# Attention's value product: high and low halves in one stationary block, one accumulator for a pair of heads

## The chip, the core and the metric

One core of a Trainium2 chip runs the whole program. Its engines are TensorE (matrix products; PE in the rows, and PEld for the loads of its stationary operand), VectorE (DVE), ScalarE (ACT), GpSimd (POOL) and SyncE (SP, which issues DMAs here). They run side by side and wait for each other through semaphores. Matmul results land in PSUM, a memory of eight banks of 2 KB in each of 128 partitions. The metric is device time of one execution in microseconds; shorter is better.

## The reference

Attention with a sigmoid in place of the softmax, its output laid out by token, then a mixture of experts with one expert per token, then a two-layer network:

```
scores = q @ k.T / sqrt(64) - log(448)        # 4 batches x 12 heads, 448 tokens, head size 64
attn   = 1 / (1 + exp(-scores))
x      = (attn @ v), heads side by side       # 1792 x 768
e(t)   = argmax over 8 of normalised x @ normalised expert_emb / tau
x      = gate * (relu(x @ w1[e]) @ w2[e])     # 1024 hidden
h      = x @ w_in                             # 2048 hidden
out    = (h - tanh(h)) @ w_out
```

All is float32. To keep its precision, the kernel splits a float32 operand into a rounded high part and the low rest ("h" and "l" in the names), and multiplies high x high, high x low and low x high, each as one fast matmul.

## The kernel before

The program has three stages: attention, experts, last network. The change is in attention, and in one step where the first expert group is prepared.

Two heads make a pair; there are 24 pairs (4 batches x 6). Keys lie on partitions with head 0 in rows 0 to 63 and head 1 in rows 64 to 127. The 448 keys of a head are three chunks of 128 and a rest of 64. The work is cut into 84 "slots" of 2 x 448 columns: slots of one pair hold chunk c of both heads; a joint slot, one to two pairs, holds the rests of both heads for both pairs. Seven slots make two pairs: three, the joint one, three.

For a slot `scores` (line 248) runs three products for each half (high x high, low x high, high x low; line 257) into a PSUM tile of two banks ("pq", three buffers, which the tiles of `rows` and of the routing share). In an ordinary slot the two heads' matmuls use 64 rows each and lie in different halves of the array. Then ScalarE takes the sigmoid twice: rounded to "ah" (line 264) and in full into pq (line 265). VectorE subtracts them to "al" (line 266), which frees pq.

`av` (line 268) multiplies values with attention. Its stationary block is 128 columns for two heads, of which a head's unit fills its own half, with zeros in the other (`vpads`, line 168, sets them). Three matmuls a unit (high values x ah, low values x ah, high values x al; line 280), seven units a pair, all into one bank "pav"; there are two such buffers. After the seventh the pair is copied out to "xT", on ScalarE for odd pairs (line 293) and on VectorE for even ones (line 295).

`rows` (line 297) turns xT so that tokens are on partitions, with four fp32 matmuls against an identity that has the normalised expert embedding beside it (`ien`, line 118), so that the routing logits come out in the same product (136 columns). VectorE adds the logits and copies the tokens (lines 313 to 316).

For each pair `prep` (line 204) lets VectorE round keys and queries in one instruction (line 217) and GpSimd subtract the low part; `prep_v` (line 222) lets GpSimd do the same for values in four.

TensorE's order is that of the program in this stage (`manual_schedule`): two slots of scores, then the value units of the two slots that lie four back, then what a table of slot numbers (`plan`, line 374) has due: `rows`, loads, preparation, routing. The other engines' orders are set by a scheduler with its own priorities; every engine runs its queue in order.

`columns` (line 779) prepares a group of 256 tokens for the experts: 12 transposes in three buffers, each copied out by ScalarE and subtracted by VectorE ("xl", line 795), then two transposes of the token numbers (line 800), for the first group into the free half of the last of these buffers.

## Time and profile before

| | |
|---|---|
| median of 3 runs | 1028.97 us (1028.47 to 1029.16) |
| profiled execution, its own time | 1029.54 us |
| span of its trace | 1027.8 us |
| TensorE busy | 1000.6 us, 97% |
| VectorE, ScalarE, GpSimd busy | 790.8, 555.8, 206.8 us |
| first and last sigmoid of the attention stage | 7.5 and 213.2 us |

How to read it: a row of the trace's order of time has the start, the duration, the engine, the line, the operation, output<-inputs, the shape of the stationary operand (rows*columns), the shape of what moves, and in brackets how long the engine had been idle and what ended that. "x2" at the end merges neighbours of one kind. A matmul's duration holds its way through the array; the next one starts before it ends, so the distance of two starts is what one costs.

### The profile page before, as it was taken

The numbers are of one execution on the slowest core, as the hardware profiler recorded it, in microseconds if no ns is written. First come the engines' busy times: TensorE is split into PE (matmuls) and PEld (weight loads), VectorE is DVE, ScalarE is ACT, GpSimd is POOL, SyncE is SP. The second block draws the span as 40 slices with busy tenths as digits, with TensorE's granted clock in tenths as the row PEclk, the third lists the DMA queues.
The fourth block names the chain that finished last, engine by engine and source line by source line (L and its number), as shares of the span: only waits on it lengthen the run. The fifth ranks groups of instructions, "written<-read, shape, count | busy, mean of one in ns | idle before, by whom it ended". The sixth has DMA issues, their size and how long they took to land.

```text
span 1027.8 us, 16784 instructions
## 1 busy us (share of the span) xinstructions
PE 1000.6 (97%) x6437; PEld 934.4 (91%) x6437; DVE 790.8 (77%) x1029; ACT 555.8 (54%) x692; POOL 206.8 (20%) x310
## 2 busy tenths in 40 slices
PE   7999999989999999999999999999999999999997
PEld 5777878779999999999999899999999999999997
DVE  7787677758859788889974888998897667766774
ACT  6788897866667666676653434344343332333230
POOL 7657677646301011100000000000001200000002
PEclk9999999999999999999999999999999999999999
DMA  6433434359658965965944555445534521233212
GB/s 173 131 89 114 128 85 123 103 196 354 239 184 301 334 228 213 305 222 184 309 152 151 195 170 180 146 179 184 192 116 154 200 107 66 104 123 117 99 62 107
DMA packets 83524, 175.26 MB, mean 171 GB/s; under 512 B 7639, under 2 KB 62958, under 8 KB 83438
## 3 DMA queue, kind: packets, MB, share of 16 engines
q1 hardware_dynamic: 79438, 155.56, 44.7%
q0 software_dynamic: 3840, 18.35, 5.0%
q8 instruction: 52, 0.85, 0.3%
q14 instruction: 34, 0.28, 0.1%
q10 hardware_dynamic: 160, 0.21, 0.1%
HBM read 156.68 MB, written 36.30 MB: 188 GB/s over the span
## 4 chain that ended last, share of the span: by engine, by line
issue 55%; PE 15%; POOL 2%; DMA 1%; DVE 1%; POOLq 0%; ACT 0%; DVEq 0%
PE pth L855 7%; PE pty L855 7%; POOL out_dram L529 2%; DMA xg<-x_tok,gidx 1%; PE xt L790 1%; DVE wl L846 0%; DVE ca L974 0%; DVE ca L972 0%; POOLq L1256 0%; DVE ca L968 0%; PE xt L800 0%; DVE hl L873 0%; ACT wi L794 0%; DVE ca L970 0%; POOLq L529 0%
## 5 line engine op out<-in xcount | busy, mean ns | idle before, releaser
L1125 PE MATMUL o<-wo,gh 128*128 128x384 f32 x896 | 240.3, 335 | 0.9 <-DVE acc L1138 0.7
L1074 PE MATMUL z<-yh,wi 128*128 128x512 f32 (+1 forms) x768 | 220.0, 365 | 0.4 <-PEq L941 0.4
L1125 PEld LDWEIGHTS o<-wo,gh 128*128 128x128 f32 x896 | 162.9, 188 | 2.5 <-DVE acc L1138 1.0
L1074 PEld LDWEIGHTS z<-yh,wi 128*128 128x128 f32 x768 | 141.6, 188 | 15.7 <-ACT yh L1049 0.6
L1125 PE MATMUL o<-wo,gl 128*128 128x384 f32 x448 | 150.0, 335 | 0.5 <-DVE gl L1099 0.5
L1074 PE MATMUL z<-yl,wi 128*128 128x384 f32 (+1 forms) x384 | 138.3, 364 | 0.0
L529 POOL DMA_INDIRECT out_dram<-acc,toki x14 | 16.7, 1193 | 572.0 <-DVE acc L1138 570.8
L266 DVE TENSOR_TENSOR al<-pq,ah 128x896 fp32r<-128x896 f32 x84 | 91.4, 1088 | 41.2 <-ACT pq L265 38.3
L855 PE MATMUL pth<-wi,wh 128*128 128x256 f32 x432 | 121.4, 282 | 0.9 <-DVE hl L873 0.9
L855 PE MATMUL pth<-wi,wl 128*128 128x256 f32 x432 | 121.1, 281 | 0.6 <-DVE wl L846 0.6
L855 PE MATMUL pth<-xl,wh 128*128 128x256 f32 x432 | 120.8, 280 | 0.0
L855 PE MATMUL pty<-hh,wl 128*128 128x256 f32 x416 | 117.1, 283 | 0.3 <-DVE wl L846 0.3
L855 PE MATMUL pty<-hl,wh 128*128 128x256 f32 x416 | 117.3, 284 | 0.0
L855 PE MATMUL pty<-hh,wh 128*128 128x256 f32 x416 | 116.9, 285 | 0.0
L1138 DVE TENSOR_TENSOR acc<-o,acc 128x768 f32<-128x768 f32 x97 | 92.4, 952 | 31.8 <-PE o L1125 31.6
L1098 ACT CAST gh<-r 128x896 fp32r<-128x896 f32 x32 | 30.1, 942 | 140.8 <-DVE r L1096 79.3
L264 ACT ACTIVATE ah<-pq,bias_s 128x896 fp32r<-128x896 f32 x84 | 85.5, 1018 | 35.9 <-PE pq L257 34.1
L846 DVE TENSOR_TENSOR wl<-w1raw,wh 128x768 fp32r<-128x768 f32 x72 | 68.5, 955 | 27.8 <-ACT wh L845 27.2
L1082 ACT ACTIVATE t<-z 128x896 f32<-128x896 f32 x32 | 29.4, 920 | 107.5 <-PE z L1074 66.2
L1125 PEld LDWEIGHTS o<-wo,gl 128*128 128x128 f32 x448 | 84.1, 188 | 2.2 <-DVE gl L1099 0.8
L845 ACT CAST wh<-w1raw 128x768 fp32r<-128x768 f32 x72 | 59.5, 834 | 44.1 <-PE pty L855 21.4
L265 ACT ACTIVATE pq<-pq,bias_s 128x896 f32<-128x896 f32 x84 | 83.0, 988 | 0.0
(269 smaller groups left out, 2221.2 us busy)
## 6 DMA issues: line engine op xcount, KB each, us to landing
w1raw<-in_moe_w_dram SPq DMA_DIRECT2D x36, 768.0 KB
w2raw<-in_moe_w_dram SPq DMA_DIRECT2D x27, 1024.0 KB
wi<-dwi SPq DMA_DIRECT2D x32, 768.0 KB
wo<-dwo SPq DMA_DIRECT2D x32, 768.0 KB
cr<-in_moe_w_in_dram SPq DMA_DIRECT2D x16, 768.0 KB
dwi<-cr SPq DMA_DIRECT2D x16, 768.0 KB
cr<-in_moe_w_out_dram SPq DMA_DIRECT2D x16, 768.0 KB
dwo<-cr SPq DMA_DIRECT2D x16, 768.0 KB
```

Of the source, the lines that this page charges most:

```text
L264: nc.scalar.activation(hi, pv, AF.Sigmoid, **sc)
L265: self.last_sig = nc.scalar.activation(pv, pv, AF.Sigmoid, **sc)
L266: nc.vector.tensor_tensor(lo, pv, f32(hi), ALU.subtract)
L529: i = self.nc.gpsimd.indirect_dma_start(**kw)
L845: nc.scalar.copy(wh, cols)
L846: self.last_split = nc.vector.tensor_tensor(wl, cols, f32(wh), ALU.subtract)
L855: self.last_mm = nc.tensor.matmul(pt[:, u], a[:, kk], b[:, kk], start=(n == 0), stop=(n == 3 * K - 1))
L1074: nc.tensor.matmul(z[:, G0[g] : G0[g] + GS[g]], wi[:, a, j * P : (j + 1) * P], yhl[half][g][b][:, j], start=(left[g] == 3 * NJ), stop=(lef ...
L1082: nc.scalar.activation(t, zv, AF.Square)
L1098: nc.scalar.copy(gv, r)
L1125: nc.tensor.matmul(o[:, w, :NW], a[:, u, i * P : (i + 1) * P], wo[:, b, w * NW : (w + 1) * NW], start=(n == 0), stop=(n == 3 * CH - 1),)
L1138: nc.vector.tensor_tensor(acc[i], ov, acc[i], ALU.add)
```

## The change

Values are kept as one tile of seven blocks of 2 x 64 columns: a block holds the high and the low part of one head's chunk side by side. A unit is now two matmuls (block x ah, block x al); the sum of high and low comes out in `rows`, whose identity is two stacked 64-wide ones. As the two heads' results would fall on the same partitions, the accumulator has two banks, one per head, and there is one buffer of it. The rests of a pair (block 6: head 0 in rows 0 to 63, head 1 in rows 64 to 127) are four matmuls of 64 rows. xT is copied by VectorE for every pair. `rows` has two 72-column matmuls for each of four chunks (one per head, overlapping in the 8 logit columns, where the second adds). The slots are taken in groups of 2, 2, 2 and 1, so that a block of value units belongs to one pair only. GpSimd prepares the values in five instructions. Three value buffers are kept for two, five plus two buffers of attention for six. The embedding is loaded in four DMAs, and its step comes two slots earlier. In `columns` the number transposes of the first group go before the last buffer is copied out.

```diff
-        pav2 = self.pool("aps3", 2, cx, space=PSUM)
+        pav2 = self.pool("aps3", 1, cx, space=PSUM)
-        NV, NW, NK = 2, 3, 3
+        NV, NW, NK = 3, 3, 3
...
+        self.et = et = cp.tile([P, 2, self.NJ, self.E], F32, name="emb_t")
+        for a in range(2):
+            for p in range(2):
+                nc.sync.dma_start(et[p * D : (p + 1) * D, a], self.emb[a * D : (a + 1) * D])
...
+        self.ien = ep.tile([P, NJ, 2, D + E], F32, name="ien")
+        eye = lambda k: self.ident[:, k * D : (k + 1) * D].unsqueeze(1).to_broadcast([P, NJ, D])
+        for a, (o, u) in enumerate(((0, D), (E, 0))):
+            nc.vector.tensor_tensor(self.ien[:, :, a, o : o + D], eye(0), eye(1), ALU.add)
+            nc.vector.tensor_tensor(
+                self.ien[:, :, a, u : u + E], et[:, a], sc[:, 0].unsqueeze(1).to_broadcast([P, NJ, E]), ALU.mult
+            )
...
+            g.tensor_copy(v[:, :6, 0], vr[:, 1:7])
+            g.tensor_tensor(v[:, :6, 1], vr[:, 1:7], f32(v[:, :6, 0]), ALU.subtract)
+            g.tensor_tensor(v[:, 6, 0], vr[:, 0], vr[:, 7], ALU.add)
+            g.tensor_tensor(vr[:, 0], vr[:, 0], f32(v[:, 6, 0]), ALU.subtract)
+            g.tensor_tensor(v[:, 6, 1], vr[:, 0], vr[:, 7], ALU.add)
...
+            groups += [(u, u + 1), (u + 2, u + 3), (u + 4, u + 5), (u + 6,)]
+            two = (0, 1)
+            blocks += [
+                [(u, two), (u + 1, two)], [(u + 2, two), (u + 3, (0,))],
+                [(u + 4, two), (u + 5, two)], [(u + 6, two), (u + 3, (1,))],
             ]
...
-            hi = sp.tile([P, 2, S], F32R, tag="ah", name="ah", bufs=LAG + 2)
+            t, nb = ("j", 2) if slots[u][0][1] == 2 else ("a", 5)
+            hi = sp.tile([P, 2, S], F32R, tag=t + "h", name="ah", bufs=nb)
...
-                for m, (vv, aa) in enumerate(((vh, hi), (vl, hi), (vh, lo))):
-                    nc.tensor.matmul(
-                        pav[:, :S], vo(vv), aa[:, x], start=(b0 and m == 0), stop=(e and m == 2)
-                    )
+                for m, t in enumerate(tiles[u]):
+                    if a < 2:
+                        nc.tensor.matmul(
+                            pav[:, a, :S], vo(slice(0, P), 3 * a + c // P), t[:, x], start=(c == 0 and m == 0), stop=False
+                        )
+                    else:
+                        for h in range(2):
+                            p = slice(h * D, (h + 1) * D)
+                            nc.tensor.matmul(pav[:, h, :S], vo(p, 6), t[p, x], start=False, stop=(m == 1))
...
-                    s["xT"] = xp.tile([P, S], F32, tag="xT", name="xT")
-                    if i % 2:
-                        nc.scalar.copy(s["xT"], pav[:, :S])
-                    else:
-                        nc.vector.tensor_copy(s["xT"], pav[:, :S])
+                    s["xT"] = xp.tile([P, 2, S], F32, tag="xT", name="xT")
+                    nc.vector.tensor_copy(s["xT"], pav[:, :, :S])
...
             for c in range(NCH):
-                o = (c % 2) * W
-                nc.tensor.matmul(
-                    pr[:CP, c // 2, o : o + W], xT[:, c * CP : (c + 1) * CP], self.ien[:, j], start=True, stop=True
-                )
+                for a in range(2):
+                    nc.tensor.matmul(
+                        pr[:, c, a * D : a * D + D + E], xT[:, a, c * CP : (c + 1) * CP], self.ien[:, j, a],
+                        start=(a == 0), stop=(a == 1), skip_group_check=True,
+                    )
...
-            plan(5, self.embedding)
+            plan(3, self.embedding, lambda: pav2.tile([P, 2, 512], F32, tag="av", name="emb_ss"))
...
+            for g, us in enumerate(groups):
+                for now[0] in us:
                     if now[0] < ns:
                         scores(now[0])
+                if g >= 2:
+                    for t in blocks[g - 2]:
+                        av(*t)
...
+            if jj == NJ // 2 - 1 and full.shape[2] >= 2 * GR:
+                pr = numbers(full[:1, 0, GR : 2 * GR])
             nc.scalar.copy(xh[:, js], pt)
```

TensorE's order around the end of a pair, before: the last value units ("vh", "vl" are the high and low values), rows, and the next slots' scores ("w" are keys and queries).

```order
L280 MATMUL pav<-al,vh_197 128x448
L280 MATMUL pav<-ah,vh_197 128x448
L280 MATMUL pav<-ah,vl_198 128x448
L280 MATMUL pav<-al,vh_197 128x448
L305 MATMUL pr<-ien,xT 112x136 x4
L257 MATMUL pq<-w0h 128x448 x2
L257 MATMUL pq<-w0l,w0h 128x448 x2
L257 MATMUL pq<-w0h,w0l 128x448 x2
```

The same place in the changed program ("v" is the tile with both parts; L283 are the half-height matmuls of the rests).

```order
L277 MATMUL pav<-ah,v_191 128x448
L277 MATMUL pav<-al,v_191 128x448
L283 MATMUL pav<-ah,v_191 128x448 x2
L283 MATMUL pav<-al,v_191 128x448 x2
L303 MATMUL pr<-ien,xT 112x72 x8
L258 MATMUL pq<-w2h 128x448 x2
L258 MATMUL pq<-w2l,w2h 128x448 x2
L258 MATMUL pq<-w2h,w2l 128x448 x2
```

Two matmuls a unit stand where three stood, the pair now ends with two couples of half height, and rows has eight matmuls of 72 columns for four of 136.

VectorE's order over some slots before, with one of its copies of xT:

```order
L266 TENSOR_TENSOR al<-pq,ah 128x896 x2
L315 TENSOR_TENSOR u<-pr,u 112x32
L316 COPY yT_last<-pr 112x4x128
L449 TENSOR_REDUCE mx<-lg 112x4
L217 TENSOR_REDUCE w1h<-kq_186 128x960
L456 TENSOR_REDUCE cm<-cand 112x4
L266 TENSOR_TENSOR al<-pq,ah 128x896
L295 COPY xT<-pav 128x448
L266 TENSOR_TENSOR al<-pq,ah 128x896 x2
```

And in the changed program (L214 is the rounding of keys and queries, L265 the subtraction of a slot):

```order
L265 TENSOR_TENSOR al<-pq,ah 128x896
L293 COPY xT<-pav 128x896
L265 TENSOR_TENSOR al<-pq,ah 128x896
L313 TENSOR_TENSOR u<-pr,u 112x32
L315 COPY yT_last<-pr 112x4x128
L265 TENSOR_TENSOR al<-pq,ah 128x896 x2
L313 TENSOR_TENSOR u<-pr,u 112x32
L315 COPY yT_last<-pr 112x4x128
L447 TENSOR_REDUCE mx<-lg 112x4
L214 TENSOR_REDUCE w1h<-kq_186 128x960
L293 COPY xT<-pav 128x896
L265 TENSOR_TENSOR al<-pq,ah 128x896
```

Every pair has its copy of xT here now, twice as wide; it stands ahead of the subtraction of the slot scored last, once of two times with the rounding right in front.

## Rows read from the trace of the kernel before

**Rows 1.** The page, busy time of an engine: us, share of the span, instructions.

```profile
PE 1000.6 (97%) x6437; PEld 934.4 (91%) x6437; DVE 790.8 (77%) x1029; ACT 555.8 (54%) x692; POOL 206.8 (20%) x310
```

**Rows 2.** Instructions of line 264: ns min/median/max, first and last start.

```profile
L264 ACT ACTIVATE ah<-pq,bias_s x84: 991/1011/1115, 7.5 to 213.2; 128x896 fp32r<-128x896 f32 x84
```

**Rows 3.** Waits from 20 to 180 us: total us, times, longest.

```profile
DVE al L266 <- ACT pq L265: 30.9, 43, 2.0
ACT ah L264 <- PE pq L257: 28.3, 21, 3.9
```

**Rows 4.** TensorE in order of time: start, duration, line, tiles, shapes.

```profile
150.90 0.47 PE L257 MATMUL pq<-w1h 128*128 128x448 f32 x1
...
152.02 0.36 PE L257 MATMUL pq<-w2h,w2l 128*128 128x448 f32 x1
152.22 0.36 PE L280 MATMUL pav<-ah,vh 128*128 128x448 f32 x1
...
154.45 0.36 PE L280 MATMUL pav<-al,vh 128*128 128x448 f32 x1
154.65 1.09 PE L305 MATMUL pr<-ien,xT 128*112 128x136 f32 x8
155.67 0.47 PE L257 MATMUL pq<-w2h 64*128 64x448 f32 x2
155.98 0.36 PE L257 MATMUL pq<-w2l,w2h 64*128 64x448 f32 x2
...
156.81 0.37 PE L257 MATMUL pq<-w2h,w2l 64*128 64x448 f32 x2
157.10 0.47 PE L280 MATMUL pav<-ah,vh 128*128 128x448 f32 x1
157.41 0.36 PE L280 MATMUL pav<-ah,vl 128*128 128x448 f32 x1
```

**Rows 5.** ScalarE in order of time, two sigmoids of one slot.

```profile
111.56 1.01 ACT L264 ACTIVATE ah<-pq,bias_s 128x896 fp32r<-128x896 f32 x1 [1.29 <-PE pq L257]
...
113.36 1.01 ACT L264 ACTIVATE ah<-pq,bias_s 128x896 fp32r<-128x896 f32 x1
```

**Rows 6.** Groups by line, loads of weights: us busy, mean ns.

```profile
L305 PEld LDWEIGHTS pr<-ien,xT 128*112 128x112 f32 x192 | 24.8, 176 | 2.6 <-issue 1.8
...
L800 PEld LDWEIGHTS xt<-ident,xg 128*1 128x1 f32 x18 | 1.4, 82 | 2.2 <-DVE xl L795 2.0
```

**Rows 7.** Groups by line from 20 to 180 us, VectorE and ScalarE.

```profile
L266 DVE TENSOR_TENSOR al<-pq,ah 128x896 fp32r<-128x896 f32 x65 | 70.8, 1089 | 31.8 <-ACT pq L265 30.9 <-issue 0.7
...
L217 DVE TENSOR_REDUCE w1h<-kq 128x960 fp32r<-128x960 f32 x7 | 8.1, 1152 | 1.4 <-DMA kq<-in_q_dram 0.5 <-DMA vr<-in_v_dram 0.4 <-issue 0.2
L316 DVE COPY rec<-pr 112x512 f32<-112x512 f32 x11 | 7.5, 681 | 0.0
...
L295 DVE COPY xT<-pav 128x448 f32<-128x448 f32 x9 | 5.6, 618 | 2.8 <-PE pav L280 2.8
L293 ACT COPY xT<-pav 128x448 f32<-128x448 f32 x9 | 5.0, 559 | 0.5 <-PE pav L280 0.5
...
L120 DVE TENSOR_TENSOR ien<-emb_t,emb_sc 128x48 f32<-128x48 f32 x1 | 1.3, 1295 | 0.0
```

**Rows 8.** VectorE in order of time, two instructions behind each other.

```profile
110.30 1.09 DVE L266 TENSOR_TENSOR al<-pq,ah 128x896 fp32r<-128x896 f32 x1 [0.70 <-ACT pq L265]
111.31 0.18 DVE L315 TENSOR_TENSOR u<-pr,u 112x32 f32<-112x32 f32 x1
```

**Rows 9.** All engines in order of time at the stage's end.

```profile
217.63 0.47 PE L280 MATMUL pav<-ah,vl 128*128 128x448 f32 x1 [0.61 <-POOL vl L235]
...
220.00 1.89 DVE L795 TENSOR_TENSOR xl<-xt,wi 128x512 fp32r<-128x512 f32 x3 [2.60 <-ACT wi L794]
...
221.94 0.38 PE L800 MATMUL xt<-ident,xg 128*1 128x128 f32 x2 [1.72 <-DVE xl L795]
```

**Rows 10.** Busy time by engine over the stage; GpSimd is POOL.

```profile
7.50:213.00 205.50, 197.33 (x1157) 160.37 (x1156) 152.24 (x249) 169.28 (x209) 138.80 (x215) 1.00 0.42 121
```

More of the change, by code (lines that the diff above doesn't have):

```diff
@@ L222, in prep_v @@
         def prep_v(i):
-            s = st[i]
-            vr = s["vr"]
-            vh, vl = vhs[i % NV], vls[i % NV]
-            flat = vr.rearrange("p a c d -> p (a c) d")
-            halves = lambda t: t.rearrange("p (a s) d -> p a s d", a=2)[:, :, 0:5:2]
-            parts = [
-                (halves(vh), halves(vl), flat[:, 1:7].rearrange("p (a s) d -> p a s d", a=2)),
-                (vh[:, 12:14], vl[:, 12:14], flat[:, 0:8:7]),
-            ]
-            for hv, lv, src in parts:
-                nc.gpsimd.tensor_copy(hv, src)
-                nc.gpsimd.tensor_tensor(lv, src, f32(hv), ALU.subtract)
-            s["v"] = (vh, vl)
-        slots = []
-        for i in range(0, n, 2):
-            ab = [[[(e, a, c * P, 6 * a + 2 * c) for a in range(2)] for c in range(3)] for e in (i, i + 1)]
-            slots += ab[0] + [[(e, 2, 3 * P, 12) for e in (i, i + 1)]] + ab[1]
+            g, s = nc.gpsimd, st[i]
+            vr = s["vr"].rearrange("p a c d -> p (a c) d")
+            v = vs[i % NV]
+            g.tensor_copy(v[:, :6, 0], vr[:, 1:7])
[3 more added lines that the diff above has]
+            g.tensor_tensor(v[:, 6, 1], vr[:, 0], vr[:, 7], ALU.add)
+            s["v"] = v
+        slots, groups, blocks = [], [], []
+        for i in range(0, n, 2):
+            u = len(slots)
+            ab = [[[(e, a, c * P) for a in range(2)] for c in range(3)] for e in (i, i + 1)]
+            slots += ab[0] + [[(e, 2, 3 * P) for e in (i, i + 1)]] + ab[1]
+            groups += [(u, u + 1), (u + 2, u + 3), (u + 4, u + 5), (u + 6,)]
[3 more added lines that the diff above has]
+                [(u + 4, two), (u + 5, two)], [(u + 6, two), (u + 3, (1,))],
+            ]
         ns = len(slots)
+        groups += [(ns, ns + 1), (ns + 2, ns + 3)]
         first = [7 * i // 2 for i in range(n)]
@@ L253, in scores @@
             for m, (kt, qt) in enumerate(((0, 0), (0, 1), (1, 0))):
-                for x, (i, a, c, _) in enumerate(slots[u]):
+                for x, (i, a, c) in enumerate(slots[u]):
                     w = st[i]["w"]
@@ L352, in attention @@
             nc.gpsimd.memset(t[:, :, self.DM :], 0.0)
+        for i in range(NV):
+            vs.append(pers.tile([P, 7, 2, D], F32R, name=f"v{i}"))
         kpads()
-        vpads()
         with tc.high_priority():
@@ L432, in attention @@
                             pass
-                u += 2
+            u = now[0] + 1
         while at:
@@ L783, in columns, with numbers @@
         xl = self.mx.tile([P, NJ, GR], F32R, tag="xl", name="xl")
+        pr = None
+        def numbers(pt):
+            for h in range(2):
+                nc.tensor.transpose(pt[:, h * P : (h + 1) * P], s["x"][:, h, self.DM : self.DM + 1], self.ident)
+            return pt
         for jj in range(NJ // 2):
@@ L796, in columns @@
         s["xt"] = (xh, xl)
-        pt = full[:1, 0, GR : 2 * GR] if full.shape[2] >= 2 * GR else pst()[:1, 0, :GR]
-        for h in range(2):
-            nc.tensor.transpose(pt[:, h * P : (h + 1) * P], s["x"][:, h, self.DM : self.DM + 1], self.ident)
+        pt = numbers(pst()[:1, 0, :GR]) if pr is None else pr
         s["row"] = self.mrow.tile([1, GR], F32, tag="row", name="row")
```

73 lines of the change are left out of this document (24 added, 49 removed).

## The prediction

> **What bounds the kernel now.** I read the page's busy shares first, then the waits of the stage that the change touches, then TensorE's own order of time there. Over the whole span TensorE is busy 97% of the time [rows 1]; that figure alone says little, since matmuls are pipelined. The change touches attention only, which runs from the first sigmoid at 7.5 us to the last at 213.2: 84 slots, 83 steps in 205.7 us, so 2.48 us a slot and, with 7 slots to two pairs, 8.67 us a pair, 24 pairs [rows 2]. In the middle of it (20 to 180 us) ScalarE waits 28.3 us for TensorE's scores, and VectorE's 30.9 us of waiting is for ScalarE, so both are fed by TensorE [rows 3]. What the reader is to see in TensorE's own rows is that they follow each other without a hole [rows 4].
>
> The price list out of these rows. One 448-column step is 0.203 us (152.22 to 154.65 is 12 of them). Two half-height (64-row) matmuls run side by side and share one such step ("x2", next start 0.2 later). A step from 64-row to 128-row operands or back costs more: 156.81 to 157.10 to 157.41 is 0.60 for two steps instead of 0.41, so 0.20 a change; likewise 155.67 to 155.98. The joint slot (the last 64 keys of both heads, both pairs) has six full matmuls, 1.22 us against 0.61 for another slot. The "rows" step (four fp32 matmuls, each recorded as two) runs from 154.65 to 155.67; less the first 0.09 of a change of height, that is 8 records at 0.116.
>
> So a pair costs TensorE: scores 3.5 x 0.61 plus half the joint slot's extra 0.61 = 2.44; values 21 x 0.203 = 4.26; rows 0.93; 14 changes of height in four pairs, 3.5 x 0.20 = 0.70. Sum 8.33, of 8.67 paid. The other 0.34 a pair is waiting, mostly round the routing steps. TensorE bounds attention; ScalarE's two sigmoids take 1.80 us a slot back to back [rows 5], 6.3 us a pair.
>
> **The change part by part.**
>
> *Values.* With high and low values as the two halves of one 128-column block, a full unit needs two matmuls (high and low attention) in place of three: 6 x 2 = 12. The joint unit becomes 2 x 2 half-height matmuls with different rows of the array, which share steps as the scores do: 2 steps. 14 steps for 21: -7 x 0.203 = -1.42 a pair. If the halves didn't share, it would be 16 steps; the scores' "x2" rows have the same form, so I take 14.
>
> *Rows.* The accumulator is now two tiles wide (one per head), and eight fp32 matmuls of 72 columns replace four of 136: 16 records for 8. Their spacing is not in the trace. Now 136 columns set 0.116; by columns alone 72 would be 0.062. But each record loads its own 112 columns of weights: such a load lasts 176 ns, one of a single column 82 [rows 6], so filling takes about 94 ns, longer than 0.062. Bounds: 16 x 0.062 = 1.0 and 16 x 0.116 = 1.86; I take 16 x 0.097 = 1.55, nearest to the loads' row, +0.62 a pair (ends +0.07 and +0.93).
>
> The Trainium skill ("TensorE: Matmul & The Clock Gate", section "LDWEIGHTS (loading the stationary operand)") gives P/1.2 ns for P columns, an estimate of 93 ns for 112; the slope of the two rows agrees (94 for 111 columns). By it rows would be 1.5 us; by the section "Back-to-back issue gap" of the same page, which goes by moving columns, the gain would be about half a microsecond a pair larger.
>
> *Changes of height.* The order of TensorE now has the half-height joint unit inside every value block of a finished pair, then full-height rows, then half-height scores. Counting round one cycle of two pairs (four groups: 2, 2, 2 and 1 slots): into and out of the four groups' scores 7 (one group follows a half-height block directly), into the two joint blocks 2, from one of them to rows 1. That is 10 in two pairs, 5 a pair for 3.5: +1.5 x 0.20 = +0.30.
>
> That is also where a rule speaks against the change: the Trainium skill ("TensorEngine Tiling (Array Packing)", section "Key Properties") says that changing the tiling mode drains the engine. The trace agrees, with 0.20 us a change; without that rule the sum would be 0.30 a pair better.
>
> TensorE's sum: -1.42 + 0.62 + 0.30 = -0.50 a pair, 7.83 in place of 8.33.
>
> *One accumulator.* The two single buffers become one double one, so a pair's first value matmul waits until VectorE has copied the pair before out. The copy is now 128x896 on VectorE for every pair (before: 128x448, alternately on ScalarE, 559 ns, and VectorE, 618 ns [rows 7]). Its price lies between the 512-column copy (681) and the 896-column subtraction from the same memory (1089); by 618 plus 448 more columns, about 1.09. VectorE issues the next instruction about 0.09 before one ends (110.30 to 111.31 for a 1.09) [rows 8], so 1.0 on its queue. VectorE's load a pair: 3.5 x 1.01 + 1.07 (rounding keys and queries) + 0.8 (rows' two copies) + 1.0 = 6.4 us, plus routing: under TensorE's 7.83 but no longer far.
>
> I walked one cycle of two pairs through these durations. Hand-over after the one-slot group: the block ends, two slots of scores (1.22) and a change of height follow, so the next block wants the accumulator 1.4 later. Wake-up is about 0.3 and the copy 1.1, if VectorE is free: wait 0 to 0.3. VectorE has the copy ahead of the subtraction of the slot just scored, which is what keeps it this short; the rounding (1.15) stands in front and is over by then. The other hand-over has rows and two slots behind it: no wait. Score buffers: three, shared with rows. The joint slot's subtraction now stands behind a subtraction, the rounding, another subtraction and the copy; in the walk it ends 9.8 to 10.25 after the cycle began, and TensorE wants that buffer at 9.55: wait 0.3 to 0.7. Together 0.3 to 1.0 in two pairs; I take 0.25 a pair, and leave the old 0.34 as it is.
>
> Attention: 24 x (-0.50 + 0.25) = -6.0.
>
> *The end and the start.* In the first expert group's transposes, the two token-number transposes now go before the copies out of the same buffer: the 1.72 us that TensorE waits at 221.94 for VectorE's "xl" goes [rows 9]; they are late by nothing else, since the data came with the others. Against it, at the end two value blocks follow each other without scores between: the one accumulator costs 0.3 + 1.1 = 1.4 there. Of the 0.61 wait for GpSimd's low values just before, the third value buffer may take away some; I count nothing. Net -0.3. At the start the embedding has one more small VectorE multiply before the first rows, 0 to 1.3 (the one of today lasts 1.3 [rows 7]), taken 0: its neighbour covers part of the wait there. GpSimd has five instructions a pair for four and has a third of its time free [rows 10]; three more small loads at the start lie ahead of keys that are not used for five slots. Neither is on the path.
>
> Sum: -6.0 - 0.3 = -6.3. Against the profiled execution (span 1027.8, its own time 1029.54) that makes 1023.2; the median of the runs shown is 0.6 lower, so 1022.6. Experts and the last network are outside the change and begin that much earlier.
>
> **The rivals.**
>
> *A. The whole saving comes (chance 0.2).* Rows go by columns (1.0 us) or the waits don't arise: -1.42 + 0.07 to 0.62 + 0.30 and little waiting, -0.5 to -0.75 a pair, -12 to -18 in all; with ScalarE and VectorE at 6.4 to 6.9 plus routing close behind, I cut it at -15: 1014 to 1017. For it: the rows step is short today. Against: the 176 ns loads.
>
> *B. No change (0.15).* Rows at 0.116 a record leave -0.19 a pair, and the walk's 0.25 eats it: -2 to +1, 1027 to 1030. For it: VectorE gets 1.0 where it had half of 0.6. Against: the loads' row.
>
> *C. Slower, through the single accumulator (0.15).* VectorE takes its queue in order, and the rounding of the next keys stands right before the copy. If the keys come late, or the rows before it do, the copy starts 1.2 to 1.6 late, and TensorE stands still at 12 hand-overs (one in each two pairs), 14 to 19 us: 1022.6 + 14 = 1037, up to 1041. It decides from 0.6 us a hand-over on (6.3 plus the bound of 2 us, over 12). For it: there is no second buffer, and the copy waits behind in-order work. Against: the walk leaves 0 to 0.3.
>
> **How the numbers follow.** Forecast 0.5: 1022.6, with its own range 1018 to 1027 (rows at 1.3 to 1.7, waits 0.15 to 0.4 a pair). A run of this kernel tells about 0.2% (2 us) from no change. Faster: all of A, 0.45 of the forecast's 0.5 and little of B, 0.67. Same: 0.15 (most of B, the forecast's upper edge). Slower: C and the upper edge of B, 0.18. The range has to reach from A's middle to the near side of C: 1014 to 1032.
>
> **What would show it.** Per pair in the middle: two value matmuls 0.203 apart, no third; joint halves as "x2"; rows' 16 records 0.09 to 0.10 apart, 1.5 us together; a step of 0.3 at 5 changes a pair; sigmoid to sigmoid 2.41 us a slot on average. TensorE's waits: on the score buffer behind the joint slot's subtraction, and under 0.3 on the accumulator. The 1.72 us before the number transposes gone, a wait of about 1.4 on the copy between the last two pairs. It is wrong if rows are above 1.9, if TensorE waits over 0.6 for the copy at each second hand-over, or if the time of a slot is set by ScalarE or VectorE with TensorE waiting at both ends.

## The result: slower, and the profile after

The changed kernel takes 1042.40 us (median of 4 runs, 1039.03 to 1044.39), the one before 1028.72 beside it: a ratio of 1.0129, interval 1.0101 to 1.0158. The forecast was 1022.6, faster than before; it came out 13.7 us slower than before. The profiled execution has a span of 1041.7 us, 13.9 longer than before. Nearly all of the loss lies in attention. Its sigmoids (columns as in [rows 2]):

```profile
L263 ACT ACTIVATE ah<-pq,bias_s x84: 992/1010/1056, 7.3 to 225.6; 128x896 fp32r<-128x896 f32 x84
```

From first to last that is 218.3 us for 205.7, 12.6 us more, so 2.63 us a slot for 2.48, and 9.20 a pair for 8.67. From the last sigmoid to the end it is 816.1 for 814.6. TensorE is no busier (the page's busy times, which answer [rows 1]):

```profile
PE 997.2 (96%) x6509; PEld 923.9 (89%) x6509; DVE 806.3 (77%) x1040; ACT 549.2 (53%) x680; POOL 210.7 (20%) x334
```

It waits more. From 20 to 180 us the waits that answer [rows 3] are:

```profile
ACT ah L263 <- PE pq L258: 38.6, 25, 9.6
DVE al L265 <- ACT pq L264: 23.3, 27, 1.6
```

ScalarE waits 10 us more for scores than before, VectorE 8 less for sigmoids: VectorE, which had been fed by the others, is now in their way. TensorE's own prices came out as forecast. In its order of time (answers [rows 4]):

```profile
106.72 0.36 PE L277 MATMUL pav<-ah,v 128*128 128x448 f32 x1
106.92 0.37 PE L277 MATMUL pav<-al,v 128*128 128x448 f32 x1
107.22 0.47 PE L258 MATMUL pq<-w1h 64*128 64x448 f32 x2
107.53 0.37 PE L258 MATMUL pq<-w1l,w1h 64*128 64x448 f32 x2
...
149.86 0.36 PE L277 MATMUL pav<-al,v 128*128 128x448 f32 x1
150.06 1.70 PE L303 MATMUL pr<-ien,xT 128*112 128x72 f32 x16
151.69 0.47 PE L258 MATMUL pq<-w0h 64*128 64x448 f32 x2
```

A value step is 0.20; the two steps round a change of height take 0.61 (106.92 to 107.53), so a change costs 0.20; and the 16 records of rows take 150.06 to 151.69; less 0.09 for the change of height that is 0.096 each. What was not in the sum are TensorE's waits from 15 to 245 us (total, times, longest):

```profile
PE pq L258 <- DVE al L265: 5.4, 8, 1.3
PE pq L258 <- DVE ro L479: 3.4, 2, 1.7
PE pr L303 <- DVE ien L127: 3.3, 1, 3.3
PE pav L277 <- DVE pe_y L599: 1.9, 1, 1.9
...
PE pav L277 <- DVE xT L293: 1.4, 2, 1.2
```

Little of it is for the accumulator (3.3 us: xT, and once behind other VectorE work, pe_y; a further 1.3 between the last pairs); most is for score buffers (the rows of pq, 13.5 us with those left out here). The second thing is in the windows: busy us (and count) of each engine, then TensorE's granted clock, the DMA share and GB/s. Before, the row of the whole stage gives 1.00 [rows 10]. (It gives 1.00 for the first microseconds of both kernels too, where steps stand 0.37 apart all the same, to 17.2 us before and to 14.2 after.)

```profile
100.00:140.00 40.00, 37.61 (x243) 28.83 (x243) 31.00 (x46) 29.45 (x35) 27.92 (x43) 0.96 0.39 111
140.00:180.00 40.00, 36.49 (x233) 28.10 (x231) 31.24 (x46) 31.45 (x39) 27.55 (x49) 0.96 0.40 119
...
38.19:45.02 6.83, 6.83 (x31) 5.39 (x32) 3.42 (x6) 1.88 (x2) 1.53 (x2) 0.50 0.39 136
72.33:79.15 6.82, 6.15 (x23) 5.26 (x24) 5.34 (x6) 3.38 (x4) 1.27 (x3) 0.50 0.32 85
103.05:106.46 3.41, 3.35 (x11) 2.65 (x12) 2.75 (x9) 2.10 (x3) 1.87 (x5) 0.50 0.46 135
157.66:161.07 3.41, 3.41 (x12) 2.56 (x10) 3.18 (x8) 1.88 (x2) 1.76 (x5) 0.50 0.40 106
```

In four stretches, 20.5 us together, TensorE ran at 0.50, the lower of its two levels (1.2 GHz). Each lies at a standstill of TensorE, counted from the start of one step to the start of the next: the second and the third begin in one (2.28 us, to 73.00, and 2.07, to 103.11), the fourth 0.7 us behind one (2.07, to 156.92), the first 1.9 us behind one (3.6, to 36.25). A fifth standstill, 2.26 us to 212.27, has no such stretch behind it: the clock is 1.00 from 180 to 260 us. Here is the third, TensorE, VectorE and ScalarE merged in order of time:

```profile
99.72 0.97 ACT L264 ACTIVATE pq<-pq,bias_s 128x896 f32<-128x896 f32 x1
...
100.36 0.24 PE L468 MATMUL prank<-oh,ones_b 112*128 112x32 bf16 x4
100.53 0.47 PE L258 MATMUL pq<-w1h 64*128 64x448 f32 x2
...
100.68 1.08 DVE L293 COPY xT<-pav 128x896 f32<-128x896 f32 x1
...
101.04 0.37 PE L258 MATMUL pq<-w1h,w1l 64*128 64x448 f32 x2
...
101.87 1.09 DVE L265 TENSOR_TENSOR al<-pq,ah 128x896 fp32r<-128x896 f32 x1
...
103.11 0.74 PE L258 MATMUL pq<-w1h 64*128 64x448 f32 x2 [1.70 <-DVE ro L479]
...
105.44 0.58 PE L277 MATMUL pav<-ah,v 128*128 128x448 f32 x1
105.81 0.58 PE L277 MATMUL pav<-al,v 128*128 128x448 f32 x1
```

The sigmoid at 99.72 is over at 100.69, so its subtraction could start; the wide copy of the accumulator stands ahead of it in VectorE's queue (100.68 to 101.76), then two routing steps. The subtraction ends at 102.96, and only then has TensorE a buffer for its next scores: 2.07 us after the step at 101.04. (The row names "ro", the last semaphore of several; the subtraction is what ends then.) The three score buffers were taken by that slot, by the ranks of the routing (prank) and by the slot of 100.53. Afterwards a step takes 0.37 instead of 0.20.

### The profile page after: what moved, and what is told of

It reads as the page before. It is cut to its first block, busy times and chain, and to the rows that moved or that the text cites. A ratio compares the mean times of both kernels' runs of the same rounds, so it can differ in the third digit from the quotient of the medians.

```text
span 1041.7 us, 16923 instructions
## 1 busy us (share of the span) xinstructions
PE 997.2 (96%) x6509; PEld 923.9 (89%) x6509; DVE 806.3 (77%) x1040; ACT 549.2 (53%) x680; POOL 210.7 (20%) x334
## 4 chain that ended last, share of the span: by engine, by line
issue 55%; PE 15%; POOL 2%; DMA 1%; DVE 0%; POOLq 0%; ACT 0%; DVEq 0%
PE pth L860 7%; PE pty L860 7%; POOL out_dram L527 2%; DMA xg<-x_tok,gidx 1%; PE xt L795 1%; DVE wl L851 0%; POOLq L1261 0%; DVE ca L977 0%; PE xt L786 0%; DVE hl L878 0%; ACT wi L801 0%; DVE ca L975 0%; POOLq L527 0%; POOLq L946 0%; DVEq L851 0%
## 5 line engine op out<-in xcount | busy, mean ns | idle before, releaser
L265 DVE TENSOR_TENSOR al<-pq,ah 128x896 fp32r<-128x896 f32 x84 | 91.1, 1086 | 31.2 <-ACT pq L264 31.0
L851 DVE TENSOR_TENSOR wl<-w1raw,wh 128x768 fp32r<-128x768 f32 x72 | 68.6, 955 | 29.3 <-ACT wh L850 29.3
L860 PEld LDWEIGHTS pth<-wi,wh 128*128 128x128 f32 x432 | 81.4, 188 | 2.6 <-issue 1.7
```

The lines of the kernel that those rows point to most:

```text
L265: nc.vector.tensor_tensor(lo, pv, f32(hi), ALU.subtract)
L851: self.last_split = nc.vector.tensor_tensor(wl, cols, f32(wh), ALU.subtract)
L860: self.last_mm = nc.tensor.matmul(pt[:, u], a[:, kk], b[:, kk], start=(n == 0), stop=(n == 3 * K - 1))
```

## The experiments

Four theories. T1: VectorE's in-order queue got the wide copy for every pair, and score buffers come back late. T2: the hand-over of the one accumulator costs by itself. T3: at the start, the first rows wait for the embedding table (ien). T4: TensorE's standing still brings its clock down, and that costs as much again. All ratios are to runs of the kernel before beside it.

### Accumulators or score buffers

One accumulator in the kernel before:

```diff
-        pav2 = self.pool("aps3", 2, cx, space=PSUM)
+        pav2 = self.pool("aps3", 1, cx, space=PSUM)
```

> The kernel before with one edit: one accumulator buffer in place of two; its copies stay 448 columns wide and alternate between ScalarE and VectorE. T2 (the hand-over itself costs): TensorE waits for the copy at half or more of the 24 hand-overs, 0.5 to 1.0 each, 6 to 20 us: 1035 to 1048. T1 (what hurts is the wide copy in VectorE's queue, not the hand-over): 1028 to 1032. T4: if hand-over waits bring pauses of 2 us, stretches at 1.2 GHz appear here too.

It measured 1057.68, ratio 1.0280 (1.0239 to 1.0320), above T2's range and T1's. The second accumulator was worth 28 us in the old order, where a pair's values followed the last pair's directly. TensorE's waits for the copy make 19.3 us of it; the clock, 0.97 from 15 to 245 us, is in it as well:

```profile
PE pav L280 <- ACT xT L293: 10.7, 5, 2.2
PE pav L280 <- DVE xT L295: 8.6, 10, 1.1
```

Two accumulators in the changed kernel, at the cost of a score buffer:

```diff
-        ps2 = self.pool("aps2", 3, cx, space=PSUM)
+        ps2 = self.pool("aps2", 2, cx, space=PSUM)
-        pav2 = self.pool("aps3", 1, cx, space=PSUM)
+        pav2 = self.pool("aps3", 2, cx, space=PSUM)
```

> The changed kernel with the memory dealt otherwise: two accumulators of two banks and two score buffers in place of one and three. T2 (the hand-over of the accumulator is what costs): the waits on xT go, 1028 to 1036. T1 (score buffers that come back late from VectorE's queue): worse, 1045 to 1075, since each score step then waits for the subtraction two slots before; the waits on xT go all the same, the waits of scores on al at least double, and T4 adds many stretches at 1.2 GHz.

It measured 1082.36, ratio 1.0515 (1.0497 to 1.0532). No wait on xT is left, and those for score buffers are four times as long:

```profile
PE pq L258 <- DVE al L265: 21.7, 17, 2.4
PE pr L303 <- DVE al L265: 11.1, 16, 1.7
```

So what is scarce is score buffers. The clock, 0.92 from 15 to 245 us here, has its part in the 40 us too. That the new order hides most of the hand-over, as planned, is seen in the changed kernel itself, where the waits for the accumulator are 3.3 us; T2 in its plain form is out there. What a second accumulator would bring without the loss of a score buffer wasn't tried.

### The copy in VectorE's queue

All copies on ScalarE:

```diff
-                    nc.vector.tensor_copy(s["xT"], pav[:, :, :S])
+                    nc.scalar.copy(s["xT"], pav[:, :, :S])
```

> The changed kernel with one edit: the 128x896 copy of the accumulator (xT) goes to ScalarE for every pair instead of VectorE. Theories: T1, VectorE's queue: the wide copy stands in VectorE's in-order queue ahead of the subtractions (al) and row copies that give the score buffers back, and TensorE stands still for them. T2, the hand-over: with one accumulator TensorE waits for that copy itself, whichever engine makes it. T3, the start: the rows of the first pair wait 3.3 us for the table of embeddings (ien). T4, the clock: pauses of TensorE of 2 us and more are each followed by 3.4 to 6.8 us at 1.2 GHz, which costs as much again. T1 expects the pauses at 71, 101, 155 and 210 us gone, with T4 three of the four stretches at 1.2 GHz too: 1027 to 1032. T2 expects no gain, 1040 to 1044, with a wait of TensorE on ACT's xT in place of DVE's. If ScalarE (1.80 us a slot, so 6.3 a pair, and 1.0 more) becomes the bound instead, 1034 to 1045 with TensorE waiting for scores to be taken. T3: the pause at 33 us stays whatever the copy does.

It measured 1041.08, ratio 1.0108 (1.0087 to 1.0129): no gain that can be told apart. The pause at the routing of the first batch shrank from 2.07 to 1.23 and the clock was 1.00 from 60 to 180 us; but the start got worse (4.8 us for ien, and a clock of 0.83 from 20 to 60), and TensorE waited 5.7 us for ScalarE's copy, in four places. Half and half:

```diff
-                    nc.vector.tensor_copy(s["xT"], pav[:, :, :S])
+                    nc.scalar.copy(s["xT"][:, 0], pav[:, 0, :S])
+                    nc.vector.tensor_copy(s["xT"][:, 1], pav[:, 1, :S])
```

> The changed kernel with one edit: the accumulator's copy is split by head, the first head's 448 columns on ScalarE and the second's on VectorE (about 0.56 and 0.62 us by the narrow copies of the kernel before). T1 (VectorE's queue): half the added load of VectorE goes, and ScalarE gets 0.56 a pair, as much as it had on average before, twice as often: 1027 to 1034. T2 (the hand-over itself): the copy takes 0.6 in place of 1.1, which shortens each wait by 0.5, at most 24 of them: 1033 to 1039, with the clock stretches that follow score-buffer waits still there. T3: the pause at 33 us and the drop of the clock behind it stay. Nothing of T1 or T2: 1040 to 1044.

It measured 1042.27, ratio 1.0113 (1.0093 to 1.0133), outside T1's range and T2's. Here the hand-over does cost, 14.3 us in 12 waits, since VectorE's half got behind a subtraction that ScalarE's half didn't wait for:

```profile
117.08 0.55 ACT L293 COPY xT<-pav 128x448 f32<-128x448 f32 x1
117.20 1.09 DVE L265 TENSOR_TENSOR al<-pq,ah 128x896 fp32r<-128x896 f32 x1 [0.29 <-ACT pq L264]
118.20 0.61 DVE L294 COPY xT<-pav 128x448 f32<-128x448 f32 x1
...
118.96 0.44 PE L277 MATMUL pav<-ah,v 128*128 128x448 f32 x1 [0.93 <-DVE xT L294]
```

T1 and T2 are two ends of one queue: if the copy goes first, a score buffer is late; if the subtraction does, the accumulator is. The old alternation, with odd pairs on ScalarE:

```diff
-                    nc.vector.tensor_copy(s["xT"], pav[:, :, :S])
+                    if i % 2 == 1:
+                        nc.scalar.copy(s["xT"], pav[:, :, :S])
+                    else:
+                        nc.vector.tensor_copy(s["xT"], pav[:, :, :S])
```

> The changed kernel with one part undone: the accumulator's copies alternate again (odd pairs on ScalarE, even on VectorE), everything else as changed. T1 (VectorE got 1.0 us a pair more in its in-order queue, which gives score buffers back late): the same gain over the changed kernel as the copy had beside the norm, 1033 to 1038. T2 (the hand-over as such): 1040 to 1044. The 3.3 us wait of the first rows, and the clock's drop behind it, stay.

It measured 1037.37, ratio 1.0064 (1.0042 to 1.0087): 6.7 us back by the ratios, 5.0 by the medians, within T1's range. With a change at the start too (the delayed values of the next part) both parities ran; the even one was on record first:

> As the one before, with odd pairs on ScalarE and even ones on VectorE (the same alternation as before the change). T1: 1027 to 1033, like the even one. T2: 1033 to 1038; a difference between the two over 3 us would say that only one of the two hand-overs of a cycle is late, the one whose engine has a subtraction or a sigmoid in front of the copy.

> The edit of the norm, and the 128x896 accumulator copies of even pairs (whose hand-over follows the one-slot group) on ScalarE, of odd pairs on VectorE. T1 (VectorE's queue sets it): half of the added load goes from VectorE without ScalarE getting more than 0.46 a pair over before: 1027 to 1033, no pause of 2 us in the middle. T2 (the hand-over waits 1 to 1.5 at each second pair whoever copies): 1033 to 1038. The all-ScalarE copy had cycles of two pairs of 17.0 to 17.9 us against 17.3 on average before, so parity with before is the best that T2 allows.

With odd pairs on ScalarE it measured 1036.06, ratio 1.0071 (1.0054 to 1.0088), with even ones 1044.68, ratio 1.0157 (1.0140 to 1.0174). It matters which hand-over gets which engine, by 8.6 us. But T1's 1027 to 1033 missed both, and the odd one can't be told from the same start without alternation (1.0082, interval 1.0066 to 1.0099, below). So the 6.7 us hold for the changed kernel's own start, not as a fixed price of the copies.

### The start

The norm of the embeddings on VectorE, but for its power:

```diff
-        self.norm_plus_eps(ss, sc[:, 0], sc[:, 1], self.mhalf[:, 0:1].to_broadcast([P, E]))
+        self.norm_plus_eps(ss, sc[:, 0], sc[:, 1], self.mhalf[:, 0:1].to_broadcast([P, E]), nc.vector)
...
-        g.tensor_tensor(r0, ss, mhalf, ALU.pow)
+        self.nc.gpsimd.tensor_tensor(r0, ss, mhalf, ALU.pow)
```

> The changed kernel with one edit: the norm of the embeddings at the start runs on VectorE but for its power, so that the table of embeddings no longer waits behind GpSimd's value splits. T3 with T4: the 3.3 us wait of the first rows at 33 us goes or falls under 1.5, and the stretch at 1.2 GHz behind it (38 to 45 us) with it: 1035 to 1039. T3 without T4 (the wait costs only itself): 1038 to 1041. If later waits take the time up (T1 and T2 set the pace over the whole of attention): 1040 to 1044. The pauses at 71, 101, 155 and 210 us stay in every case.

It measured 1039.11, ratio 1.0099 (1.0071 to 1.0128), inconclusive: ien came in time, but the two small multiplies that make it took 2.2 us (below), and TensorE stood 3.3 us for a subtraction behind them and a rounding. Then GpSimd was made to finish the norm before the values of pairs 1 to 3:

```diff
+            if 1 <= i <= 3:
+                with tc.issue_after(self.norm_ins.ins):
+                    split_v(i)
...
```

> The changed kernel with one edit: GpSimd makes the whole norm of the embeddings before it goes on with the value splits of pairs 1 to 3 (in the earlier run the norm on VectorE only moved the wait into VectorE's queue: TensorE stood 3.6 us for a score buffer at 29 us instead). T3 (the late table costs its 3.3 us) with T4 (the pause brings 6.8 us at 1.2 GHz): both go, 1035 to 1038. T3 without T4: 1038 to 1041. T2 (the later waits take it all up, or the delayed value splits are waited for instead): 1040 to 1044. The pauses behind score buffers and the accumulator stay.

It measured 1038.24, ratio 1.0082 (1.0066 to 1.0099). Its profile doesn't bear out the theory's way: TensorE waited 6.9 us for the delayed values instead, with 10.2 us at 1.2 GHz in that wait and behind it.

Last, both: the short steps on VectorE, the power on GpSimd before the low keys of pair 2, then the values in order of use, and the copies alternating.

```diff
...
+            plan(3, self.embedding, lambda: pav2.tile([P, 2, 512], F32, tag="av", name="emb_ss"))
+            plan(3, behind, prep, 2)
...
```

> The alternating copies, and a start in which nobody waits: the embeddings' norm on VectorE but for its power, which GpSimd takes before the low keys of the third pair and the splits of the second pair's values (these in the order of use). T3 with T4: neither the 3.3 us wait for the table nor one of 2 us or more on values, no stretch at 1.2 GHz before 60 us; against the alternating copies alone 6 to 9 us less, 1026 to 1031. T3 without T4: 3 less, 1031 to 1035. If the start's pauses only move to another buffer once more: 1034 to 1038.

It measured 1031.25, ratio 1.0012 (1.0001 to 1.0024), 5 to 6 us under the alternation alone. From 15 to 60 us these waits are left, and no stretch at the lower clock between 20 and 100:

```profile
PE pq L258 <- DVE al L265: 3.0, 3, 1.4
PE pav L277 <- DVE xT L296: 0.5, 1, 0.5
```

The time lies on the border of two ranges, T3 with T4 (to 1031) and T3 without (from 1031); the traces decide. In the alternation's, TensorE waits 4.6 us for ien, and the 21st sigmoid starts at 61.12; here it starts at 53.87, 7.25 us sooner. So more than the wait itself came back, and T3 with T4 holds. GpSimd, busy 20% of the span, was the late one: in the changed kernel its norm of eight small steps was strewn among value and key splits, from 14.1 to 35.7 us.

### The clock

Work in place of a pause, in the changed kernel; the products aren't used:

```diff
+FILLER = 10
...
+        for k in range(FILLER if b < self.B - 2 else 0):
+            nc.tensor.matmul(
+                full[:, 1, :384], self.ones_b, self.ones_b.unsqueeze(1).to_broadcast([CP, 3, P]),
...
```

> The changed kernel with work added: behind the routing's matmuls of the first two batches TensorE multiplies ones into an unused half of the same buffer, ten times 384 columns, some 1.6 us at full clock, where it otherwise stood still for 2.06 us. The result isn't used. T4 (TensorE's standing still there brings the clock down): the stretches of 3.4 us at 1.2 GHz at 103 and 158 us go, and the kernel with more work is faster by 2 x (1.7 to 2.8) us: 1036 to 1040. Without T4 the stretches stay, and the time is that of the changed kernel or up to 3 us over it: 1041 to 1046.

It measured 1037.88, ratio 1.0071 (1.0053 to 1.0090): by the medians 4.5 us faster with more work than the changed kernel, and the intervals are apart. First the filled pause in order of time, then the windows in which the clock had been 0.96:

```profile
102.08 0.24 PE L470 MATMUL prank<-oh,ones_b 112*128 112x32 bf16 x4
102.18 1.78 PE L476 MATMUL prank<-ones_b 112*128 112x384 bf16 x10
103.89 0.47 PE L259 MATMUL pq<-w1h 64*128 64x448 f32 x2
```

```profile
100.00:140.00 40.00, 39.11 (x263) 29.39 (x259) 32.84 (x50) 30.29 (x36) 28.07 (x44) 1.00 0.37 111
140.00:180.00 40.00, 38.04 (x253) 28.79 (x253) 32.61 (x47) 32.88 (x41) 28.74 (x51) 1.00 0.42 123
```

T4 is shown for these two places: with work in the pauses' place, the two stretches of 3.41 us are gone. Round the first place (34th to 43rd sigmoid) the profiled execution took 23.82 us for 25.32 before, round the second (55th to 64th) 23.72 for 25.29. That is 3.1 us together, as much as 6.82 us lose when a step takes 0.37 in place of 0.20; the rest of the 4.5 us isn't placed. On the version with alternating copies and the better start, the same work at three batches:

> The alternating copies and the start without waits, and the added work (ten matmuls of ones by 384 columns behind the routing's own) at the first three batches, the routing where it was. T4: the stretches at 1.2 GHz at 146 and 191 us go, 1.7 to 2.8 us each, and where a pause of 2.2 us was, nothing else changes: 1025 to 1029. If the clock falls all the same: 1030 to 1033.

It measured 1028.08, ratio 0.9985 (0.9976 to 0.9995), 3 us under it. One stretch at the lower clock is left, from 198 to 201 us, behind another standstill (2.4 us, to 197.30, for the accumulator).

### The routing

Ranks in spare columns of the accumulator instead of a score buffer:

```diff
-                pr = lambda: ps1.tile([P, 2, 512], F32, tag="qk", name="prank")
+                pr = lambda: self.pav[:, :, S:]
```

> As the one before, and the ranks of the routing (prank, 40 columns) go into spare columns of the accumulator in use instead of taking one of the three score buffers. If it is the third score buffer that is missing at those places (T1's form: buffers come back after subtraction, copy and routing in VectorE's order), the pauses of about 2 us behind the routing's matmuls at two places go, and with T4 the stretches at 1.2 GHz behind them: 2 to 6 us under the one before, 1022 to 1028. If VectorE's queue as such is full there (the accumulator's copy and seven routing steps ahead of a subtraction): within 1 us of it.

It measured 1030.11, ratio 1.0001 (0.9991 to 1.0011), inconclusive: at that place the accumulator is the next pair's, so the ranks now waited for the copy (3.2 us in two waits on VectorE, 2.1 in one on ScalarE). Then the place alone:

```diff
-ROUTE, ROUTE_E = 8, 3
+ROUTE, ROUTE_E = 9, 3
```

> The alternating copies and the start without waits, and the routing of the first two batches planned one slot later: its matmuls then stand behind a value block in the middle of a pair, two slots of scores away from a copy of the accumulator. If the pauses of 2.2 us there (88 and 140 us) come of two things that meet, the copy and the routing in VectorE's queue and the ranks in a score buffer, they shrink to 1 us or less, and the stretch at 1.2 GHz behind one of them goes: 2 to 5 us less, 1026 to 1029. If one of the two is enough for the pause: 1030 to 1032.

It measured 1027.00, ratio 0.9979 (0.9968 to 0.9990): faster than before the change. The two pauses fell from 2.2 to 1.3 us, and the clock is 1.00 from 20 to 180 us. The copy, the ranks and the routing's VectorE steps had to meet at one place for a pause of that length. Both edits:

> As the routing one slot later, with its ranks in spare columns of the accumulator as well: there the accumulator is in use already, so that the ranks no longer wait for the copy of the pair before (in the earlier run that wait, 1.6 to 2.1 us at three places, took the place of the one it removed). If the score buffer that the ranks take is still a cost: 0.5 to 2 us under the routing one slot later, 1025 to 1028. If the place alone was: within 0.5 of it.

It measured 1024.13, ratio 0.9949 (0.9932 to 0.9966). This one changes values: the ranks begin a group of their own in a bank in which a head's sum is half done. The Trainium skill ("PSUM — Partial Sum Buffer", section "The four PSUM rules") says that the second group's first matmul then makes the first group's next one overwrite its sum. So only its time is used.

### What is left

ScalarE's squares one to a slot for the first two batches, and that with the third batch's squares and routing moved as well:

```diff
- plan(now[0] + 1 + c // 2 if b < B - 1 else now[0], square, bt, c)
+ plan(now[0] + (0 if b == B - 1 else 1 + c // 2 if b == B - 2 else 1 + c), square, bt, c)
```

> As the routing one slot later, and ScalarE's squares of the first two batches go one to a slot of scores instead of two. What is left in the steady part are waits of about 1.0 (two batches, once each) behind the joint slot, whose sigmoids stand behind two squares (0.85 each). If those squares are the cause, both waits fall under 0.4: 1 to 2 us less, 1025 to 1026.5. If the waits move to the next slot: no difference, 1026.5 to 1027.5.

> As the one before with the squares of the third batch spread too, and that batch's routing two slots later, behind a value block in the middle of a pair. The pauses of 1.06 and 1.52 us at 184 us (scores behind the routing's matmuls) shrink to half: 1 to 2 us less, 1023.5 to 1025.5. If the first expert group, whose rows are fetched after that routing, then starts late (TensorE waits for them at the end of attention): 1026 to 1031.

The first measured 1026.97, ratio 0.9970 (0.9958 to 0.9982): nothing that can be told apart, the waits moved on. The second measured 1033.30, ratio 1.0031 (1.0016 to 1.0047), 6.3 us more; 4.2 of them are TensorE's waits for the first expert group's rows (xg), which came late at the transposes. Last, with the squares one to a slot, the ranks in the accumulator without a start of their own, for the first two batches:

```diff
-                    plan(now[0] + ROUTE, self.route_b, b, r, pr)
+                    plan(now[0] + ROUTE, self.route_b, b, r, lambda: self.pav[:, :, S:], False)
```

> As the squares one to a slot, and the ranks of the first two batches in spare columns of the accumulator in use, without a start of their own (the pair's first value matmul has started the bank); the third batch's stay in a score buffer. If the score buffer that the ranks take costs the 1.3 us pauses that are left at the two routings: 1 to 3 us less, 1023 to 1026, which would be the forecast's 1022.6 but for the end. If the queue of VectorE alone makes them: within 1 us of the one before, 1026 to 1028.

It measured 1024.84, ratio 0.9957 (0.9943 to 0.9970): the best version, 4.4 us (0.43%) under the kernel before. Its interval overlaps that of the squares alone, so what the ranks' place is worth by itself isn't clear.

The way there, by ratios, each step on top of the one before: changed 1.0129; copies alternate 1.0064; start 1.0012; routing one slot later 0.9979; squares and ranks 0.9957. The forecast had been 0.994.

## Why the prediction was wrong

**TensorE's sum was right.** Values, rows and changes of height measured 0.20, 0.096 and 0.20, as forecast (0.203, 0.097, 0.20); the rows' records go by their loads, not by their columns (0.062). Where nothing stands in the way the pace follows. Two sigmoids seven slots, so two pairs, apart in the version with the routing one slot later:

```profile
40.33 1.01 ACT L263 ACTIVATE ah<-pq,bias_s 128x896 fp32r<-128x896 f32 x1 [0.36 <-PE pq L258]
...
56.17 1.01 ACT L263 ACTIVATE ah<-pq,bias_s 128x896 fp32r<-128x896 f32 x1 [0.35 <-PE pq L258]
```

That is 15.84 us, 7.92 a pair; the sum said 7.83. It is a best case: 15.8 to 15.9 comes back a few times in the stage, but the middle one of all such distances is 17.25, and the average pair takes 8.48. Of the 0.50 a pair, this version got 0.19.

**The step that failed is "One accumulator": waits of 0.25 a pair.** Against the sum, attention pays 9.20 - 7.83 = 1.37 a pair where 0.25 + 0.34 were set, 0.78 too little, 19 us over 24 pairs. TensorE's waits between the first and the last sigmoid add up to 8.0 us before (its largest row is below), which is the old 0.34 a pair, and to 22.4 after.

```profile
PE pq L257 <- DVE al L266: 4.2, 6, 1.5
```

So the change added 14.4 us of waits where 24 x 0.25 = 6.0 were set. With -12.0 for TensorE's sum and at most 9.3 for the clock (below) that makes 11.7 of the 12.6 us that attention grew by. The hand-over itself is nearly as walked: 1.4 us in two waits, and 1.9 once, at 210 us, where other routing work stands before the copy. But the walk counted "VectorE has the copy ahead of the subtraction of the slot just scored" as what keeps the wait short, and left out who pays for it: the subtraction, and with it a score buffer, is 1.2 late. It also walked one cycle without routing, whose ranks take one of the three score buffers and whose steps go into the same queue. Putting the copies back to two engines gave 5 to 6.7 us, moving the routing, later, 3 to 4.

**The clock was in no step.** The prediction took a wait to cost its length. In four stretches TensorE did at 0.37 a step what takes 0.20: 20.5 us x (1 - 0.203/0.373) is 9.3 us at most. The two stretches of 3.41 us, 3.1 us by this reckoning, measured 3.1 us where work filled their pauses. The Trainium skill ("TensorE: Matmul & The Clock Gate", section "What's actually happening") has it that activity releases the clock and idling throttles it to 1.2 GHz; the 0.50 in all four rows agrees.

**The start, set at 0 of "0 to 1.3".** The bound was too narrow: TensorE waits 3.3 us in place of the 1.5 of before, and the clock's first 6.8 us stretch lies behind it. VectorE's multiplies weren't it (0.2 us each). The first rows, before and after:

```profile
37.96 2.08 PE L305 MATMUL pr<-ien,xT 128*112 128x136 f32 x16 [1.45 <-DVE ien L120]
```

```profile
36.25 4.54 PE L303 MATMUL pr<-ien,xT 128*112 128x72 f32 x32 [3.26 <-DVE ien L127]
```

TensorE's last step ahead of them starts at 32.63 for 36.14, 3.5 us sooner; the table is there 1.7 us sooner only, though GpSimd begins its norm 6.4 us sooner (14.10 for 20.51). In between GpSimd makes key and value splits almost without a pause. The prediction called it "not on the path" by its free time over the whole stage. How much of this a pair's fifth value instruction makes (0.3 us each) no run separates. With the start repaired, 5 to 6 us came back.

**The end, forecast -0.3, came out at +1.5** (816.1 against 814.6). The 1.72 us before the number transposes is gone, and the hand-over between the last pairs costs 1.5, both as written; the first expert matmul comes 10.7 us behind the last sigmoid, for 13.2 before. But this group, sooner begun, waits for VectorE. TensorE's waits from 210 to 330 us, before and after:

```profile
PE pth L855 <- DVE hl L873: 0.9, 1, 0.9
...
PE pth L855 <- DVE wl L846: 0.6, 1, 0.6
...
```

```profile
PE pth L860 <- DVE hl L878: 1.5, 1, 1.5
...
PE pty L860 <- DVE wl L851: 1.2, 1, 1.2
...
```

With the rows left out, the waits within the expert group are 3.5 us for 1.8. The last network then waits 1.6 us for its weights (DMA), which it did not before.

**The rivals.** C came nearest in place (one accumulator, VectorE in order) and in time (1037 to 1041). That its time is so near is luck, since the clock, up to 9.3 us, is in the measured time, and its mechanism was not the one: it had the copy late, twelve times 1.2 to 1.6. The split copy shows that mechanism as written, 14.3 us in 12 waits; the changed kernel has the copy early and the buffers late. A and B hung on the rows step at 0.062 or 0.116 a record; it measured 0.096. Of the three signs of being wrong only the last came, and in places only: VectorE sets the time of a slot, with TensorE waiting.

What stays open: the last 2 us to the forecast. The best version still waits 4.3 us for subtractions in five places; that VectorE's queue is all of it wasn't tried. Its clock is 0.96 from 20 to 60 and from 180 to 220 us, too.

## What to carry to other kernels

When a buffer is given up, walk the whole in-order queue of the engine that frees it, also for the buffers that the same queue frees: a copy that comes in time makes something else late. Walk the worst place of the loop, where side work meets (here copy, routing and ranks), not the plain cycle, since a pause of 2 us there can cost 1.5 us more through the clock (measured, at the two filled places), and by the step times 3.1 where the stretch behind it is 6.8 us long. A third score buffer can be worth more than a second accumulator.

## What the runs showed of the hardware

A pause of TensorE of 2 us was often, not always, followed by the lower clock (of the changed kernel's five, one was not). In the kernel with the norm on VectorE two pauses at the same place of the loop, 2.07 us (scores at 98.18, next at 100.25) and 2.04 us (150.51, next at 152.55), differ in it:

```profile
98.00:106.00 8.00, 6.28 (x38) 4.50 (x34) 7.03 (x15) 5.92 (x7) 5.93 (x7) 1.00 0.33 95
150.00:158.00 8.00, 6.32 (x32) 4.32 (x29) 6.71 (x17) 4.47 (x6) 5.96 (x10) 0.79 0.29 79
```

Runs of the changed kernel spread by 5 us (1039.03 at a mean clock of 0.992, 1044.39 at 0.984), where the four of the kernel before beside them lay within 0.7. That such pauses make this spread isn't shown: in later rounds the kernel before spread from 1028.4 to 1032.3 as well.

A small VectorE instruction with two inputs can last as long as a GpSimd one beside it. The multiply of 128x48 that makes ien, first in the changed kernel, then with the norm on VectorE, and GpSimd's instruction beside the last of it:

```profile
L127 DVE TENSOR_TENSOR ien<-emb_t,emb_sc x2: 200/204/207, 36.0 to 36.1; 128x48 f32<-128x48 f32 x2
```

```profile
L127 DVE TENSOR_TENSOR ien<-emb_t,emb_sc x2: 1029/1150/1272, 28.1 to 29.3; 128x48 f32<-128x48 f32 x2
```

```profile
29.28 0.99 POOL L225 TENSOR_TENSOR v<-vr,v 128x384 fp32r<-128x384 f32 x1
```

0.20 us became 1.03 and 1.27; the last starts with GpSimd's (29.3) and ends with it. The Trainium skill ("SBUF — State Buffer", section "🔬 SBUF: two separate sides") says that the two engines share a pair of ports as an exclusive lock, for VectorE instructions with two inputs from there; the rows agree. The 1.3 us of this multiply before the change [rows 7] may have been the same: it ran from 36.52 to 37.81, beside GpSimd's low parts of keys, 35.37 to 37.75.
